# Output, gate and up weights loaded as adjacent rows, with head outputs regrouped on TensorE

## The chip, the cores and the metric

The kernel runs on one core of a Trainium2 chip. A core has TensorE (PE) for matrix products, VectorE (DVE), ScalarE (ACT), GpSimd (POOL) and SyncE (SP), each with its own instruction stream that runs in order, and 16 DMA engines that move data between main memory and the on-chip buffers. Products land in PSUM banks, and everything else lies in SBUF, a memory of 128 partitions. The metric is the device time of one execution in microseconds (us). Three runs of the kernel before took 267.55, 268.86 and 269.77 us.

## The reference: two decoder layers for one token of four sequences

Each of the four rows of x (512 values) passes twice through the same attention block and the same feed-forward block. Both layers use the same weights and the same key and value caches.

```python
B, Sq, D = 4, 1, 512
Hq, Hkv, Sk, Dh = 32, 8, 4096, 128
D, F = 512, 1792
def _A_ref(x, k_cache, v_cache, wq, wo):
    q = (x @ wq) split into 32 heads of 128
    scores = q . k * Dh ** -0.5          # four query heads share one cache head
    o = softmax(scores) . v
    return o.reshape(B, Sq, Hq * Dh) @ wo
def _B_ref(x, w_gate, w_up, w_down):
    return (_gelu(x @ w_gate) * (x @ w_up)) @ w_down

x = x + _A_ref(_layernorm(x), k, v, wq, wo)
x = x + _B_ref(_layernorm(x), w_gate, w_up, w_down)
x = x + _A_ref(_layernorm(x), k, v, wq, wo)
x = x + _B_ref(_layernorm(x), w_gate, w_up, w_down)
```

A sequence's keys are 8 heads of 4096 x 128 in bf16, 1 MB a head, and its values are as large. All in all 64 MB of caches are read at least once, and 13.25 MB of weights: wq and wo with 4 MB each, gate, up and down with 1.75 MB each.

## The kernel before: how the work is tiled, staged and ordered

**Order of the sequences.** The kernel interleaves the layers. `attend_first` runs the attention of layer 1 for sequence 0. Then, for each sequence b, a dense block (`dense_first` or `dense`) runs layer 1's feed-forward part, and `attend` runs layer 2's attention of b, whose keys are still in SBUF, beside layer 1's attention of b+1, whose keys arrive meanwhile. For the last sequence `attend_last` does layer 2's attention alone. The output projection, the feed-forward part of layer 2 and the result (`dense_last`) are done for all four sequences together at the end. So there are four passes with layer-1 attention (the first, and three `attend`) and one last pass.

**Tiles.** A head of a cache is two tiles of 128 partitions x 16 x 128 values (512 KB, 4 KB a partition). Keys are kept whole for a sequence (tiles `kw`, `kp`), and are transposed in place by DVE (L537). Value tiles go through a ring of eight slots (`v_t`): each step of class `Values` uses one tile (`step`, L828), frees its slot, and lets SP issue the next load (`pump`, L708). A few value tiles are kept from layer 1 for layer 2.

**Attention.** `scores` (L592) multiplies keys by a spread query, `soft` takes the softmax over DVE and ACT, `soft_swap` (L647) turns the probabilities on PE, with an ACT copy behind (L650). Values are multiplied in one of two ways: with the tile as weights (L859, output `ot`), or with the probabilities as weights (`stream_v`, L791, output `so`), which DVE then transposes (L799), sums (L806) and scales (L807) into `OT_bf` (layer 1) or `OT2_bf` (layer 2; the profile cuts digits off and writes OT_bf for both). `ot` outputs need one scaling operation (L680). `Values.scale` is that work on DVE; `hold=True` puts it off until `flush`.

**The output projection.** `OT_bf` holds one column a query head, with the 128 values of the head on the partitions. `wo_sb` holds, for head i, the 128 rows of wo that belong to it (`wo_dram`, L102). For most heads `RowProj.heads` (L405) has the head's column as weights and a row block of 512 as moving data, which gives rows; `split` (L412, L413) brings these into bf16 and `onto` adds them through PE to the output `y`. For the last heads `OutProj.heads` (L388) has wo as weights and gives columns. `heads` are four groups of eight query heads, that is, pairs of cache heads, in the order in which they are used.

**What sets the order.** The order of every engine's instructions is that of the program text, written out by hand (`manual_schedule`): `attend_first` (L959), `attend` (L1135) and `attend_last` (L1252) say which step follows which. `busy` (L482) issues filler matmuls whose result nobody reads. All large loads are issued by SP, in program order. `load_rest` (L158) issues wo in four transfers, gate, up and down behind the first pass's values; the first feed-forward block and the keys of sequence 1 follow.

**The dense blocks.** x lies in `xb` and `XX` with 512 = 4 x 128 as (block k, partition p). Gate, up and q have x as weights and a row block of the weight as moving data (L309, L1323, L1390); a DVE transpose (L315) turns rows into columns. In `dense_last`, `row` adds the residual x (and what bf16 cut from it) into `xr` through the identity, and L1440 multiplies down.

## Time and profile before

| | |
|---|---|
| median of three runs | 268.86 us (267.55 to 269.77) |
| the profiled execution's own time | 268.99 us |
| its span, first to last instruction | 267.2 us |
| mean granted TensorE clock | 0.866 of full |
| bytes read | 102.5 MB, 384 GB/s over the span |
| busy: PE, DVE, ACT, POOL | 195.1, 182.2, 66.0, 3.9 us |
| wo: four transfers of 1 MB, rows of 1 KB | 11.0 to 12.9 us from issue to landing |
| packets under 2 KB / all | 7144 / 30732 |

Rows of the timeline read: start, duration (both us), engine, line, operation, output <- inputs, shape, count, and in brackets the idle time of the engine before it and what ended it. Neighbouring instructions of one kind are merged, so a duration can cover short pauses. PEld is the loading of weights, which overlaps PE. Windows give, for each stretch, its length, the busy time of PE, PEld, DVE, ACT and POOL with counts, the granted clock, the DMA engines' busy share and GB/s. The rows of 40 slices cut the span into slices of 6.68 us.

### The profile page before, as it was taken

What the parts mean: (1) busy time and instruction counts of PE and PEld (TensorE: products, weight loads), DVE (VectorE), ACT (ScalarE), POOL (GpSimd) and SP (SyncE); (2) the same over time, 40 slices, a digit from 0 to 9 for tenths busy, and PEclk for the clock granted to TensorE, in tenths of its full rate; (3) what the DMA queues carried; (4) which work ended last, traced back from release to release, by engine and by line L of the source; (5) the groups of instructions that cost most, each with busy time, mean ns of one, the idle gap of its engine ahead of it and who ended that gap; (6) DMA issues with size and microseconds to landing.
All of it is one profiled execution on the core that took longest, in us unless ns stands there. A gap on an engine that the chain in (4) does not pass through costs nothing.

```text
span 267.2 us, 8596 instructions
## 1 busy us (share of the span) xinstructions
PE 195.1 (73%) x3767; PEld 114.8 (43%) x3775; DVE 182.2 (68%) x448; ACT 66.0 (25%) x136; POOL 3.9 (1%) x10
## 2 busy tenths in 40 slices
PE   1396246544689796989678968787788687888884
PEld 1333123322255453557436245464363354553563
DVE  3385955451335899884776998746769996568773
ACT  1001001100222422032323520304136103044642
POOL 2000000000001000000000000000000000000001
PEclk9998555655597959799999985899999979999999
DMA  7999999999994999999999999999999999999940
GB/s 244 432 416 421 423 429 417 408 385 406 413 412 177 394 416 417 420 417 400 390 414 416 416 419 421 416 415 375 403 418 418 421 415 418 420 405 405 413 160 3
DMA packets 30732, 103.05 MB, mean 386 GB/s; under 512 B 2788, under 2 KB 7144, under 8 KB 29672
## 3 DMA queue, kind: packets, MB, share of 16 engines
q1 hardware_dynamic: 30672, 102.51, 95.7%
q8 instruction: 29, 0.48, 0.6%
q14 instruction: 7, 0.06, 0.1%
q10 hardware_dynamic: 24, 0.01, 0.0%
HBM read 102.50 MB, written 0.00 MB: 384 GB/s over the span
## 4 chain that ended last, share of the span: by engine, by line
DMA 51%; PE 21%; DVE 16%; SPq 6%; ACT 3%; issue 3%; DVEq 0%
DMA v_t<-in_A_v_cache_dram 25%; DMA kp<-in_A_k_cache_dram 8%; DMA kw<-in_A_k_cache_dram 8%; PE sc L592 6%; DMA wu_sb<-in_B_w_up_dram 5%; DMA kw<-in_A_v_cache_dram 4%; SPq L161 4%; DVE kp L537 3%; PE ot L859 3%; DVE kw L537 3%; PE y L275 3%; PE so L791 2%; PE q L309 1%; DVE q L315 1%; DVE qb L360 1%
## 5 line engine op out<-in xcount | busy, mean ns | idle before, releaser
L592 PE MATMUL sc<-kw,qb 128*32 128x512 bf16 x244 | 39.6, 446 | 5.2 <-DVE kw L537 2.2
L592 PE MATMUL sc<-kp,qb 128*32 128x512 bf16 x268 | 40.1, 450 | 1.0 <-DVE kp L537 0.2
L592 PEld LDWEIGHTS <-qb 128*32 128x32 bf16 x512 | 23.1, 104 | 39.6 <-issue 21.4
L537 DVE STREAM_TRANSPOSE kw<-kw 128x1024 f32<-128x1024 f32 x32 | 38.0, 1215 | 0.7 <-DMA kw<-in_A_k_cache_dram 0.6
L537 DVE STREAM_TRANSPOSE kp<-kp 128x1024 f32<-128x1024 f32 x32 | 36.7, 1199 | 0.0
L859 PE MATMUL ot<-pe,v_t 128*128 128x32 bf16 (+1 forms) x896 | 30.0, 184 | 5.6 <-DMA v_t<-in_A_v_cache_dram 2.8
L859 PEld LDWEIGHTS <-v_t 128*128 128x128 bf16 x896 | 27.7, 100 | 13.7 <-issue 7.4
L614 ACT ACTIVATE pe<-sc,nl 128x512 bf16<-128x512 f32 x8 | 5.5, 687 | 85.9 <-DVE pe L611 67.6
L791 PE MATMUL so<-v_t,pe 128*32 128x256 bf16 x304 | 15.0, 319 | 13.6 <-DMA v_t<-in_A_v_cache_dram 11.6
L799 DVE STREAM_TRANSPOSE so<-so 128x512 f32<-128x512 f32 (+1 forms) x23 | 13.8, 599 | 11.1 <-PE so L791 11.1
L791 PEld LDWEIGHTS <-pe 128*32 128x32 bf16 x320 | 9.1, 105 | 19.4 <-issue 12.5
L602 DVE TENSOR_REDUCE pe<-sc 128x1 f32<-128x512 f32 x12 | 8.3, 691 | 9.2 <-PE sc L592 9.1
L405 PE MATMUL yr<-wo_sb,OT_bf 128*2 128x512 bf16 (+1 forms) x120 | 10.7, 425 | 4.9 <-DMA wo_sb<-in_A_wo_dram 4.9
L647 PE MATMUL x<-pe,ident_bf 128*32 128x128 bf16 x192 | 5.4, 233 | 11.8 <-DVE pe L622 11.8
L647 PEld LDWEIGHTS <-ident_bf 128*32 128x32 bf16 x256 | 5.3, 100 | 16.1 <-issue 14.1
L791 PE MATMUL so<-v_t,pl 128*32 128x256 bf16 x192 | 9.4, 275 | 3.3 <-DMA v_t<-in_A_v_cache_dram 3.3
L650 ACT CAST pe<-x 128x512 bf16<-128x512 f32 x12 | 7.0, 586 | 17.4 <-PE x L647 17.4
L275 PE MATMUL q<-xb,wq_sb 128*128 128x5 bf16 (+1 forms) x192 | 5.7, 173 | 6.5 <-DMA wq_sb<-in_A_wq_dram 6.5
L353 PE MATMUL qe<-q_bf,ident_bf 128*32 128x16 bf16 (+1 forms) x272 | 5.7, 176 | 5.6 <-DVE q_bf L335 2.9
L622 DVE STREAM_TRANSPOSE pe<-pe 128x512 bf16<-128x512 bf16 x12 | 8.4, 696 | 1.1 <-ACT pe L614 1.1
L275 PEld LDWEIGHTS <-wo_sb 128*128 128x128 bf16 x160 | 7.6, 101 | 3.3 <-DMA wo_sb<-in_A_wo_dram 2.6
L482 PEld LDWEIGHTS <-ident_bf 128*128 128x128 bf16 x63 | 5.2, 99 | 8.7 <-issue 4.3
(172 smaller groups left out, 255.2 us busy)
## 6 DMA issues: line engine op xcount, KB each, us to landing
v_t<-in_A_v_cache_dram SPq DMA_DIRECT2D x89, 512.0 KB, 8.5
kp<-in_A_k_cache_dram SPq DMA_DIRECT2D x32, 512.0 KB, 9.9
kw<-in_A_k_cache_dram SPq DMA_DIRECT2D x24, 512.0 KB, 9.6
wq_sb<-in_A_wq_dram SPq DMA_DIRECT2D x2, 2048.0 KB, 7.7
kw<-in_A_k_cache_dram SPq DMA_DIRECT2D x4, 1024.0 KB, 11.6
v_t<-in_A_v_cache_dram SPq DMA_DIRECT2D x4, 1024.0 KB, 14.2
wo_sb<-in_A_wo_dram SPq DMA_DIRECT2D x4, 1024.0 KB, 12.0
wq_sb<-in_A_v_cache_dram SPq DMA_DIRECT2D x3, 1024.0 KB, 11.8
```

The lines of the kernel that those rows point to most:

```text
L161: dq.dma_start(out=wo_sb[:, i * n:(i + 1) * n], in_=wo_dram[:, i * n:(i + 1) * n])
L275: nc.tensor.matmul(dst, lhsT=lhsT, rhs=rhs, start=first, stop=last, skip_group_check=True)
L405: nc.tensor.matmul(self.rows[j:j + x.shape[1]], lhsT=x, rhs=wo_sb[:, i], start=self.n < QD, stop=True, skip_group_check=True)
L537: nc.vector.transpose(out=words, in_=words)
L592: nc.tensor.matmul(sc[s * QS:(s + 1) * QS], lhsT=qb[:, w0:w0 + 2 * W], rhs=kt[:, :, be // 2, :, be % 2], start=(t == 0 and be == 0), stop= ...
L602: nc.vector.tensor_reduce(out=m, in_=sc.rearrange("p c j -> p (c j)"), axis=AX.X, op=ALU.min if norm else ALU.max)
L622: nc.vector.transpose(out=flat, in_=flat)
L647: nc.tensor.matmul(x[a * QS:(a + 1) * QS, s], lhsT=ident_bf[:, s * QS:(s + 1) * QS], rhs=pT[:, a], start=True, stop=True, skip_group_check ...
L650: nc.scalar.copy(out=pe, in_=x.rearrange("p s t c h -> p (s t c h)"))
L791: nc.tensor.matmul(ps[d, :NW * QS], lhsT=x[:, w:w + NW].rearrange("p c h -> p (c h)"), rhs=v[:, i:i + NW, d], start=first and i == 0, stop ...
L799: nc.vector.transpose(out=flat, in_=flat)
L859: nc.tensor.matmul(self.ot[:, s % 2], lhsT=v[:, i, :], rhs=wide(pe[:, s, t * CH + i, :], self.ot.shape[-1]), start=(done == 0 and i == 0), ...
```

## The change

Loads of wo, gate, up and wq are cut differently, and the order of values in x changes with them.

- In `load_rest`, the output weights of half of the cache heads (those with head mod 4 below 2, two of the four transfers) load with four adjacent rows of wo (4 KB) for a partition: partition p holds rows 4p to 4p+3 of the 512 rows of a cache head's four query heads. The other two transfers stay as they are.
- For those heads the outputs have to lie the same way. A new `Values.regroup` does this: for j in 0 to 3 and each of the four query heads, a matmul of every fourth column of the identity against the head's column writes 32 partitions in PSUM, and an ACT copy brings the result back into `OT_bf` or `OT2_bf`. That is 16 matmuls and a copy for a pair of cache heads. It is called twice in each pass: ahead of the softmax, and between steps or row groups further on.
- Gate and up load with two adjacent rows (7 KB) a partition. So x is kept as (block of 256, partition, even or odd): the out projection and the first pass's down read their weights with a stride of two (`every_other`), later down blocks are read as pairs (`adjacent`), and the residual in `dense_last` is put together from even and odd halves (16 matmuls of 64 columns for 8 of 128). wq loads in two transfers for each half of the heads, its pieces 4 KB as before.
- Some calls change places: in `attend` the third group's rows come in one piece behind the regroup, a filler of five and one of three swap, and in `attend_last` the rows' sum goes between the two halves of the last heads.

```diff
     def load_wq(g):
         n = HG * Dh
-        dq.dma_start(out=wq_sb[g][:], in_=wq_dram[:, :, g * n:(g + 1) * n])
+        for k in range(KD // 2):
+            dq.dma_start(out=by_pairs(wq_sb[g][:])[:, k], in_=wq_dram[:, k, :, g * n:(g + 1) * n])
 
     def load_rest():
         n = Hq // 4
-        for i in range(4):
-            dq.dma_start(out=wo_sb[:, i * n:(i + 1) * n], in_=wo_dram[:, i * n:(i + 1) * n])
-        dq.dma_start(out=wg_sb[:], in_=B_w_gate.rearrange("(k p) n -> p k n", p=P))
-        dq.dma_start(out=wu_sb[:], in_=B_w_up.rearrange("(k p) n -> p k n", p=P))
+        wo_quads = A_wo.rearrange("(i p j) n -> p i j n", p=P, j=QD)
+        to_quads = wo_sb.rearrange("p (i j) n -> p i j n", j=QD)
+        for kvh in range(0, Hkv, 2):
+            if by_quads(kvh):
+                dq.dma_start(out=to_quads[:, kvh:kvh + 2], in_=wo_quads[:, kvh:kvh + 2])
+            else:
+                i = kvh * rep
+                dq.dma_start(out=wo_sb[:, i:i + n], in_=wo_dram[:, i:i + n])
+        dq.dma_start(out=by_pairs(wg_sb[:]),
+                     in_=B_w_gate.rearrange("(k p e) n -> p k e n", p=P, e=2))
...
     class OutProj / RowProj
-                    mac(self.full[:, k], wo_sb[:, i, k * P:(k + 1) * P],
+                    mac(self.full[:, k], wo_sb[:, i, every_other(k)],
...
+        def regroup(self):
+            kvh, n = self.due[0][1][0], sum(len(unit) for _, unit in self.due)
+            ps = self.due[-1][0]
+            self.due = []
+            ...
+            for j in range(QD):
+                for h in range(rep):
+                    nc.tensor.matmul(turned[h * QS:(h + 1) * QS, :, j], lhsT=ident_bf[:, j::QD],
+                                     rhs=o[:, :, h], start=True, stop=True, skip_group_check=True)
+            nc.scalar.copy(out=o, in_=turned)
+
         def scale(self, ot, unit, rden):
             n, s = len(unit), unit[0] % GH
+            if self.quads is not None and by_quads(unit[0]):
+                self.due.append((ot, unit))
...
     attend_first
         vals.step(3, hold=True)
+        vals.regroup()
         p0 = soft(sc1)
...
-        vals.step(TG)
-        assert vals.left() == 0
+        vals.step(2 * NT + 1)
+        vals.regroup()
+        vals.step(vals.left())
         load_rest()
...
     attend
         scores(sc1, gy, 1, last_alone)
+        vals1.regroup()
         p0 = soft(sc1)
...
-        rows.heads(heads[2], rep)
+        vals1.regroup()
+        busy(5, spare)
+        vals1.step(1)
+        rows.heads(heads[2], hp)
+        rows.split()
         busy(3, spare)
-        vals1.step(1)
-        rows.heads(heads[2] + rep, rep)
-        rows.split()
-        busy(5, spare)
         vals1.step(1)
...
     attend_last
+        vals.regroup()
         vals.step(4)
         rows.heads(heads[0], hp)
         rows.heads(heads[1], hp)
+        vals.regroup()
         vals.step(2)
...
         vals.step()
+        proj.n = Hq - rep
+        proj.heads(heads[3] + rep, rep // 2)
         rows.onto(proj)
-        proj.n = Hq - rep
-        proj.heads(heads[3] + rep, rep)
+        proj.heads(heads[3] + rep + rep // 2, rep // 2)
...
     dense_last
         for x in (xb[:], xlo):
             for k in range(KD):
-                row(xr, k, x[:, k, :B], ident_bf[:])
+                half = slice(k % 2 * P // 2, (k % 2 + 1) * P // 2)
+                for e in range(2):
+                    row(xr, k, x[:, k // 2 * 2 + e, :B], ident_bf[:, half], slice(e, P, 2))
```

More of the change, by code (lines that the diff above doesn't have):

```diff
@@ L967, in attend_first @@
                       streamed=[h for h in range(Hkv) if h != last],
-                      paired=[h for h in range(Hkv) if h // 2 != last // 2])
+                      paired=[h for h in range(Hkv) if h // 2 != last // 2],
+                      quads=OT_bf.unsqueeze(2))
         ring.extend(1, b, one(b))
```

36 lines of the change are left out of this document (26 added, 10 removed).

## The prediction

> **What bounds the kernel now.** I read the DMA rows of the page first, then the chain that ended last, then the same time in windows of 2 us, then the timelines of single engines where the diff edits.
>
> ```profile
> DMA  7999999999994999999999999999999999999940
> GB/s 244 432 416 421 423 429 417 408 385 406 413 412 177 394 416 417 420 417 400 390 414 416 416 419 421 416 415 375 403 418 418 421 415 418 420 405 405 413 160 3
> ...
> DMA 51%; PE 21%; DVE 16%; SPq 6%; ACT 3%; issue 3%; DVEq 0%
> ```
>
> The 16 DMA engines are full from 6.7 us to about 256 us, with one hole (slice 13, 80.6 to 84.3 us). So the time is bytes over rate, plus that hole, plus an opening, plus a tail of some 9 us after the last bytes. Only three things can pay: a better rate, a shorter hole, a shorter tail. Work on PE, DVE or ACT elsewhere costs nothing until it makes DMA run dry.
>
> The rate is not the same everywhere. In windows of 2 us (the last two columns are the DMA share and GB/s):
>
> ```profile
> 48.00:50.00 2.00, 1.63 (x34) 1.08 (x34) 0.26 (x1) 1.02 (x2) 0.00 (x0) 0.75 1.03 416
> ...
> 56.00:58.00 2.00, 0.94 (x8) 0.23 (x9) 2.00 (x5) 0.00 (x0) 0.00 (x0) 0.50 1.09 386
> ```
>
> The second window is wo arriving in rows of 1 KB; the first is cache tiles in rows of 4 KB. The engines are as busy or busier, and move 7% less. PE's timeline gives the price exactly, since each group starts as its quarter of wo lands:
>
> ```profile
> 57.06 1.02 PE L405 MATMUL yr<-wo_sb,OT_bf 128*2 128x512 bf16 x8 [1.62 <-DMA wo_sb<-in_A_wo_dram]
> 59.76 1.02 PE L405 MATMUL yr<-wo_sb,OT_bf 128*2 128x512 bf16 x8 [1.68 <-DMA wo_sb<-in_A_wo_dram]
> 62.44 1.02 PE L405 MATMUL yr<-wo_sb,OT_bf 128*2 128x512 bf16 x8 [1.65 <-DMA wo_sb<-in_A_wo_dram]
> 65.16 1.11 PE L275 MATMUL y<-OT_bf,wo_sb 128*128 128x64 bf16 x16 [1.70 <-DMA wo_sb<-in_A_wo_dram]
> ```
>
> 2.70 us a quarter (1.049 MB): 388 GB/s. The gate lands at 69.59 and up at 73.94 (starts of their first readers): 4.43 and 4.35 us for 1.835 MB each, 414 and 422 GB/s, in rows of 3.5 KB.
>
> **What it saves: 0.45 us.** Two quarters of wo go to rows of 4 KB, as the cache tiles have, at 418 GB/s (the steady windows): 2.51 instead of 2.70 us each, 0.4 us for two. Gate and up in rows of 7 KB are bounded by nothing below and by 422 GB/s above: 0.1 us for the gate at most, and I take 0.05. All this lies ahead of the landing of up, from which the chain runs through the first feed-forward block and the first scores to the loads that end the hole. So the hole keeps its length and all behind it comes 0.45 us earlier. The trace has no 4 KB row of wo. Bounds: 0, if the row length is not what costs, and 0.55, at 422 GB/s for all four transfers. The value is nearest to the cache tiles, which have the same row.
>
> The Trainium skill ("DMA: Bandwidth & Descriptors", Specifications) sets line rate at 512 B and up, by which 1 KB rows would lose nothing and this saving would be zero. 388 against 418 GB/s speaks against that. The same page ("Why small descriptors are slow") gives some 3 cycles of overhead for each packet beside one for each 32 B: 35 cycles for 1 KB and 131 for 4 KB, 6% less by an estimate from the page, close to the 7% here.
>
> **What is moved at no cost.** Loading wq in two halves of rows that stay 4 KB: two SP issues more, some 0.45 us each (L156), at the very start, past the key loads and the second half of wq behind them. DMA has over 4 us of work ahead of each. Nothing is gained, since the q matmuls need both halves. Weights read with a stride of two (out projection, down): the trace has such loads for the up projection (LDWEIGHTS of wu_sb, 96 ns) beside contiguous ones of wo_sb (98 ns); equal. Down rows read with a stride: gate rows (strided) take 0.95 us for 16x448, q rows (contiguous) 1.06 us for 16x512; equal for a column. The output's residual rows become 16 matmuls of 64 columns instead of 8 of 128: PE is idle for 0.40 us just behind them (before L1440 at 263.18), and eight more fit (the 56 of that line took 0.95, 0.02 each).
>
> **The regroup, by itself.** 16 matmuls of ident_bf against 2 to 8 columns, then one ACT copy. The nearest row is the spread of q:
>
> ```profile
> 133.25 0.27 PE L353 MATMUL qe<-q_bf,ident_bf 128*32 128x16 bf16 x16 [0.63 <-DVE q_bf L335]
> ```
>
> 0.27 us a regroup. The copy: 0.16 us (L1417, 128x4) to 0.27 us (L1464, 128x128); I take 0.2. What matters is what PE waits for, since PE runs in order and the regroup reads what DVE has just scaled. There are two in each attention pass of layer 1 and two in the last pass.
>
> First pass: the first lies ahead of a 2.03 us idle stretch of PE (45.5 to 47.5), the second after five tiles, ahead of a tile that lands at 51.84, while DVE ends that pair at 51.37. Free.
>
> Passes 2 to 4, first regroup: 0.27 us between scores and fillers, behind which PE is idle 0.78 to 0.97 us for the turned softmax (L647). Its input was ready (L680 at 165.6 against scores' end at 167.5). Free. Second regroup: in the passes that end at 180 and 235 us DVE has ended the second head (175.09, 230.09) as PE gets there, and PE then runs 0.27 of regroup and 0.65 of filler where it had 0.33 of rows and 0.42 of filler, up to a tile at 176.24 and 231.21. Free within 0.1 us. In the pass that ends at 125 us PE arrives at 120.17, DVE ends at 120.46: 0.3 wait, 0.27 of work and the longer filler put the out projection some 0.55 us later. Behind it PE waits on transfers anyway (0.73 at 128.28, 0.59 at 130.83), issued with 5.5 us of other transfers ahead of them. I take 0.1 us for all three; bounds 0 and, if nothing is absorbed, 3 x 0.57 = 1.7.
>
> **The regroups in the last pass: +1.7 us.** Here nothing covers them.
>
> ```profile
> 253.08 0.40 PE L627 MATMUL den<-zx,masks 128*128 128x16 f32 x2
> 253.83 1.06 PE L791 MATMUL so<-wq_sb,pl 128*32 128x256 bf16 x32 [0.36 <-ACT pl L650]
> 254.71 1.04 PE L405 MATMUL yr<-wo_sb,OT_bf 128*4 128x512 bf16 x16
> 255.84 0.62 PE L791 MATMUL so<-wq_sb,pl 128*32 128x256 bf16 x16
> 256.29 0.60 PE L405 MATMUL yr<-wo_sb,OT_bf 128*4 128x512 bf16 x8
> 257.04 0.57 PE L859 MATMUL ot<-pl,kw 128*128 128x32 bf16 x16 [0.15 <-DMA kw<-in_A_v_cache_dram]
> ```
>
> ```profile
> 253.67 0.72 DVE L799 STREAM_TRANSPOSE so<-so 128x512 f32<-128x512 f32 x1
> 254.43 0.22 DVE L806 TENSOR_REDUCE ov<-so 128x8 f32<-128x64 f32 x1
> 254.68 0.18 DVE L807 TENSOR_TENSOR OT_bf<-ov,rden 128x8 bf16<-128x8 f32 x1
> ...
> 259.54 0.18 DVE L425 TENSOR_TENSOR xb<-XX,y 128x16 bf16<-128x16 f32 x1 [0.63 <-PE y L275]
> ```
>
> The first regroup stands ahead of the four V tiles that now start at 253.83. It needs DVE's L807, done at 254.86. Queued behind it on PE: those tiles, then all the rest. On the old clock, with each offset taken from the lines above:
> - regroup 254.9 to 255.2; four tiles start at 255.2 (+1.35); both row groups end at 257.1. The ACT copy sits behind the table load (254.45 to 255.73) and is done by 256.0, in time.
> - DVE scales the next pair from 256.3 for the 1.21 us that it took (254.94 to 256.15): 257.5. So the second regroup waits 0.4 and ends at 257.8. In the kernel before, this scaling lay beside rows and the next tiles.
> - next tiles at 257.75, rows 258.2 to 258.8, DVE's scaling of that head (0.67 after the tiles begin, 0.9 long) ends at 259.3, out projection of it from 259.35; last V tile 259.8 to 260.3; the split of the rows on ACT and DVE (1.1 and 1.7 after the tiles begin, 2.3 until done) ends at 260.2, so the last scale runs from 260.3 to 260.5.
> - 16 matmuls of out projection took 0.59 from start to their DVE reader; with the four of the rows now between them 0.72: xb at 261.3 instead of 259.54.
>
> That is +1.75 us. The cover that the old order had, waits on the last transfers (0.59, 0.66 and 0.21 us on PE, at 255.84, 257.04 and 258.32), is used up in this sum: DMA ends no later, so no term is left for it. Moving the rows' sum behind half of the last heads is 0.1 of it. Bounds: 0.6 us, if only PE's added work and the swapped order stay (2 x 0.27 + 0.1), and 2.2, if the copies come late too (2 x 0.2).
>
> **Sum.** -0.45 + 0.1 + 1.75 = +1.4 us. The profiled execution took 268.99 us with a span of 267.2, so 1.8 lies around the span; 268.99 + 1.4 = 270.4. The median of the three runs shown is 268.86, 0.13 lower; I forecast **270.3 us**, 0.5% slower.
>
> **Rivals.**
> - **The wide rows bring nothing** (the rate of wo comes from elsewhere). Then the saving goes: 270.7. For: the engines' busy share rises to 1.09 in that window without a cause named. Against: gate and up run at 414 to 422 in the same stream. Chance 0.12.
> - **PE's delays reach the transfers.** V loads wait on PE for a free slot; if the second regroup of passes 2 to 4 delays the freed slots and the queue then runs short, each pass loses up to 0.57 us and with the first regroup's 0.27, 0.84: 3 x 0.84 = 2.5 in place of 0.1, 272.7. It decides once a pass loses 0.45 us of transfer time: 1.25 more in all, and over 1% slower. For: the rate sags just there (336 GB/s at 132 us, 295 at 184). Against: 5.5 us of transfers are queued there. Chance 0.13.
> - **Not slower: the hole shortens.** From 79.9 to 83.0 us the granted clock is 0.50, with PE busy all 3.1 us on q and the first scores, on whose end the next loads wait. Had PE the full clock there, as it has from 73 to 79.9, 1.55 us would go and the sum would be -0.15: 268.8. It decides from 1.4 us on, nine tenths of that stretch. For: the drop comes under full load, so its place is not fixed by the work in it. Against: the order of work ahead of it hardly changes. Chance 0.10. The Trainium skill ("TensorE: Matmul & The Clock Gate", Part 1) describes a free-running window of activity of 3.4 us, by which a shift of the work by 0.45 us could fall either way; no run here shows that.
>
> The forecast keeps 0.65. **Range:** from 268.4 (the shortened hole and the low tail cost) to 272.3 (most of the way to the second rival, and the tail's upper bound with no saving: 268.9 + 2.2 + 0.1 = 271.2). The three runs before spread over 2.2 us, so 1% (2.7 us) is about what tells a difference from none. Over 1% slower, above 271.55: the second rival and the upper edge of the tail cost, 0.17. Faster than 266.2: 0.03. Within 1%: 0.80.
>
> **What would show it.** PE's groups that read wo should start 2.5 us apart after the two wide quarters, and 2.7 after the others; up's first reader 0.45 us earlier, and the hole as long as before. In the last pass PE should idle over 1 us ahead of the first regroup with DVE's L807 as its releaser, and the last bytes should land some 0.4 us earlier while xb (add_x) comes over 1 us later. It is wrong if PE does not stall there, if the GB/s row sags more at the passes' ends, or if the granted clock in the hole differs.

## The result: 1.4% slower, not 0.5%

The changed kernel took **272.4 us** (median of six runs, 271.99 to 274.36) against 268.42 us for the kernel before (six runs on the same chip, 267.55 to 270.39): 1.0142 of its time, 95% interval 1.0109 to 1.0174, so 3.8 us more with an interval of 2.9 to 4.7. The forecast was 270.3 us, 1.4 us more. The direction was right, the size was not, and the time lies just above the range. The profiled execution took 274.36 us, span 272.5; it is the slowest of the six, so where its last pass is read, a second profiled execution (272.52 us, span 270.6) stands beside it.

The page of the changed kernel, rows DMA and GB/s of the 40 slices (6.81 us each) and the engines' shares of the chain that ended last:

```profile
DMA  6999999999994999999999999999999999999910
GB/s 155 423 419 420 424 425 419 417 404 414 417 388 168 367 416 417 417 417 417 331 405 419 416 420 417 417 417 405 407 420 415 417 417 418 417 384 385 412 48 3
...
DMA 47%; PE 21%; DVE 18%; SPq 7%; ACT 4%; issue 2%; DVEq 0%
```

The middle is what it was: full, one hole in slice 13. The first slice is new: 155 GB/s where the kernel before had 244. And the bytes end further from the end of the span: 48 GB/s in the second last slice instead of 160, 1.8 us by (160 x 6.68 - 48 x 6.81) / 418.

The two windows again, cache tiles and then wo (length; busy PE, PEld, DVE, ACT, POOL; granted clock; DMA share; GB/s):

```profile
50.00:52.00 2.00, 1.63 (x30) 1.19 (x34) 0.26 (x1) 0.56 (x1) 0.00 (x0) 0.57 1.04 418
58.00:60.00 2.00, 1.02 (x8) 0.23 (x9) 2.00 (x5) 0.00 (x0) 0.00 (x0) 0.50 1.08 406
```

And PE's timeline where the quarters of wo land:

```profile
58.96 1.02 PE L424 MATMUL yr<-wo_sb,OT_bf 128*2 128x512 bf16 x8 [1.47 <-DMA wo_sb<-in_A_wo_dram]
61.52 1.02 PE L424 MATMUL yr<-wo_sb,OT_bf 128*2 128x512 bf16 x8 [1.54 <-DMA wo_sb<-in_A_wo_dram]
64.08 1.02 PE L424 MATMUL yr<-wo_sb,OT_bf 128*2 128x512 bf16 x8 [1.54 <-DMA wo_sb<-in_A_wo_dram]
66.79 1.10 PE L294 MATMUL y<-OT_bf,wo_sb 128*128 128x64 bf16 x16 [1.69 <-DMA wo_sb<-in_A_wo_dram]
```

The quarters that load wide are the first and the third. The third lands 2.56 us after the second (2.49 to 2.56 in the traces of ten executions with wide quarters), where it took 2.68 (2.68 to 2.76 in the eight traces with narrow ones): the saving is there. But the first of these lines comes 1.90 us later than before (57.06): the delay was made ahead of it.

### The profile page after: what moved, and what is told of

Same layout as the page of the kernel before. It is cut to its first block, busy times and chain, and to the rows that moved or that the text cites. A ratio compares the mean times of both kernels' runs of the same rounds, so it can differ in the third digit from the quotient of the medians.

```text
span 272.5 us, 8954 instructions
## 1 busy us (share of the span) xinstructions
PE 195.4 (72%) x3935; PEld 118.4 (43%) x3943; DVE 182.4 (67%) x448; ACT 67.7 (25%) x146; POOL 3.9 (1%) x10
## 4 chain that ended last, share of the span: by engine, by line
DMA 47%; PE 21%; DVE 18%; SPq 7%; ACT 4%; issue 2%; DVEq 0%
DMA v_t<-in_A_v_cache_dram 29%; DMA kp<-in_A_k_cache_dram 7%; PE sc L611 5%; DMA wd_sb<-in_B_w_down_dram 4%; DVE kp L556 4%; DMA kw<-in_A_k_cache_dram 4%; PE so L810 4%; PE ot L879 3%; DVE kw L556 3%; DMA wq_sb<-in_A_wq_dram 3%; PE y L294 2%; SPq L175 2%; PE yr L424 1%; SPq L188 1%; DVE q L334 1%
## 5 line engine op out<-in xcount | busy, mean ns | idle before, releaser
L611 PE MATMUL sc<-kp,qb 128*32 128x512 bf16 x268 | 39.3, 435 | 1.0 <-DVE kp L556 0.2
L424 PE MATMUL yr<-wo_sb,OT_bf 128*2 128x512 bf16 (+1 forms) x120 | 11.4, 466 | 4.5 <-DMA wo_sb<-in_A_wo_dram 4.5
L666 PE MATMUL x<-pe,ident_bf 128*32 128x128 bf16 x192 | 5.1, 226 | 12.2 <-DVE pe L641 12.0
L666 PEld LDWEIGHTS <-ident_bf 128*32 128x32 bf16 x256 | 5.0, 98 | 16.5 <-issue 11.9
L294 PEld LDWEIGHTS <-wq_sb 128*128 128x128 bf16 x192 | 5.4, 101 | 9.1 <-DMA wq_sb<-in_A_wq_dram 8.7
L922 ACT CAST OT_bf<-so 128x8 bf16<-128x8 f32 (+1 forms) x7 | 1.2, 172 | 32.5 <-DVE pe L626 16.4
L810 PEld LDWEIGHTS <-pl 128*32 128x32 bf16 x240 | 5.6, 96 | 8.2 <-issue 6.4
```

The lines of the kernel that those rows point to most:

```text
L294: nc.tensor.matmul(dst, lhsT=lhsT, rhs=rhs, start=first, stop=last, skip_group_check=True)
L424: nc.tensor.matmul(self.rows[j:j + x.shape[1]], lhsT=x, rhs=wo_sb[:, i], start=self.n < QD, stop=True, skip_group_check=True)
L611: nc.tensor.matmul(sc[s * QS:(s + 1) * QS], lhsT=qb[:, w0:w0 + 2 * W], rhs=kt[:, :, be // 2, :, be % 2], start=(t == 0 and be == 0), stop= ...
L666: nc.tensor.matmul(x[a * QS:(a + 1) * QS, s], lhsT=ident_bf[:, s * QS:(s + 1) * QS], rhs=pT[:, a], start=True, stop=True, skip_group_check ...
L810: nc.tensor.matmul(ps[d, :NW * QS], lhsT=x[:, w:w + NW].rearrange("p c h -> p (c h)"), rhs=v[:, i:i + NW, d], start=first and i == 0, stop ...
```

## The opening: where 1.7 us went

Windows of 1 us of three kernels. The kernel before:

```profile
3.00:4.00 1.00, 0.43 (x16) 0.34 (x13) 0.47 (x3) 0.00 (x0) 0.00 (x0) 1.00 0.91 365
4.00:5.00 1.00, 0.00 (x0) 0.00 (x0) 0.19 (x2) 0.00 (x0) 0.69 (x1) 1.00 1.03 418
5.00:6.00 1.00, 0.00 (x0) 0.00 (x0) 0.16 (x1) 0.00 (x0) 0.33 (x1) 1.00 1.03 426
```

The changed kernel:

```profile
3.00:4.00 1.00, 0.38 (x15) 0.29 (x12) 0.49 (x3) 0.00 (x0) 0.00 (x0) 1.00 0.94 176
4.00:5.00 1.00, 0.00 (x0) 0.00 (x0) 0.16 (x1) 0.00 (x0) 0.74 (x1) 1.00 0.83 229
5.00:6.00 1.00, 0.00 (x0) 0.00 (x0) 0.16 (x1) 0.00 (x0) 0.28 (x1) 1.00 0.90 254
```

The experiment `wq_by_e` (below), the changed kernel with another cut of wq's two transfers:

```profile
3.00:4.00 1.00, 0.45 (x16) 0.37 (x14) 0.44 (x3) 0.00 (x0) 0.00 (x0) 1.00 0.89 328
4.00:5.00 1.00, 0.00 (x0) 0.00 (x0) 0.21 (x2) 0.00 (x0) 0.67 (x1) 1.00 1.04 422
5.00:6.00 1.00, 0.00 (x0) 0.00 (x0) 0.16 (x1) 0.00 (x0) 0.36 (x1) 1.00 0.99 406
```

The last two columns are the reading: the DMA engines of the changed kernel are 83 to 94% busy and move 48 to 60% of the bytes that the kernel before moves. They do not wait for an instruction; their packets, pieces of 4 KB in both kernels, take longer. The first MB, which is the first transfer of wq, is slow, and the second transfer behind it runs at 410 GB/s and more. The table gives GB/s in windows of 1 us for the kernels in which the start was varied, and the bytes that had landed by 10 us (sum of the ten windows). `key_first` and `wq_by_e` are made from the changed kernel, so their ratios hold the rest of the change too.

| kernel, first transfer of wq | 2-3 | 3-4 | 4-5 | 5-6 | 6-7 | 7-8 | MB by 10 us | ratio to before, 95% |
|---|---|---|---|---|---|---|---|---|
| before: all rows of a half of the heads, 2 MB | 90 | 365 | 418 | 426 | 418 | 451 | 3.09 | 1 |
| after: rows 0-255, 1 MB | 176 | 176 | 229 | 254 | 274 | 410 | 2.38 | 1.0142 (1.0109 to 1.0174) |
| `wq_split`: rows 0-255 | 156 | 254 | 262 | 225 | 344 | 418 | 2.57 | 1.0066 (1.0030 to 1.0101) |
| `wq_rev`: rows 256-511 | 156 | 229 | 303 | 221 | 365 | 418 | 2.62 | 1.0083 (1.0053 to 1.0114) |
| `wq_rows`: rows 0-255, then their other columns | 152 | 246 | 283 | 213 | 348 | 401 | 2.52 | 1.0056 (0.9975 to 1.0136) |
| `wq_two`: rows 0-255 and 256-511 from two queues | 119 | 332 | 283 | 258 | 348 | 418 | 2.64 | 1.0110 (1.0011 to 1.0209) |
| `key_first`: 1 MB of keys, then rows 0-255 | 214 | 442 | 389 | 406 | 307 | 213 | 2.78 | 1.0101 (1.0072 to 1.0129) |
| `wq_alt`: rows 0-127 and 256-383 | 173 | 418 | 414 | 414 | 426 | 447 | 3.15 | 1.0038 (0.9983 to 1.0092) |
| `wq_by_e`: every second row | 188 | 328 | 422 | 406 | 430 | 447 | 3.12 | 1.0042 (1.0004 to 1.0080) |
| `wq_cols`: all rows, half as many columns | 141 | 399 | 420 | 399 | 418 | 434 | 3.13 | 0.9989 (0.9955 to 1.0024) |

The changed kernel is 0.70 MB behind at 10 us, which is 1.7 us at 418 GB/s, and its second execution (`after_again`) 0.67 MB. Most of that is carried to the last pass: in `after_again` the first key load behind the hole is issued 1.56 us later than before (84.66, before 83.10), and the probability swap of the last pass starts 1.59 us later (254.32, before 252.73).

## The experiments

Line numbers of kernels made from the changed one can be one or two higher than there. All ratios are to the kernel before, run on the same chip in the same batch.

### The whole change again, and the last pass's regroups

`after_again` is the changed kernel unedited. `last_none` leaves out both regroups of `attend_last`, `last_late` moves them to where their input should be ready. `last_none` so leaves out the reordering of layer 2's outputs for the heads with wide weights.

> The changed kernel once more, unaltered, for a second profile. Its first profile lost 2.0 us in the opening (the first q products ended at 12.5 us instead of 10.4, DMA at 176 to 274 GB/s from 2 to 7 us) and was the slowest of six executions (274.36 against a median of 272.4). If the opening belongs to the kernel (wq in two transfers for each half), the first q products end near 12.5 us again. If it was that execution's own, they end near 10.4 us and the span is some 2 us shorter, near 270.5. The tail should be the same in both: from the start of the last probability swap on PE to the last add onto xb 9.3 us, against 6.8 us before.

> Leaves out both regroups of the last pass, so the layer-2 output projection uses columns in the wrong order for half of its heads; all transfers, all other work and the other regroups stay. If the last pass's regroups cost what the first profile shows (2.5 us between the last swap and the add onto xb), the time falls to 270.0 us (272.4 - 2.5). If they cost what was forecast, 1.75 us: 270.7 us. If the loss lies in the opening and in the passes: 272 us. The trade of places between the rows' sum and the last heads stays in, so the swap-to-add stretch should be 6.9 us.

> Both regroups of the last pass put one step later: the first behind the four value tiles (whose scaling is held until then), the second behind the next two. The sum done is the same. If the cost of the regroups is PE's wait on DVE, it falls: the first regroup finds DVE done (254.86 against PE there at 254.9 in the kernel before), and the rows of the second group wait some 0.3 us for the table load and copy, so some 0.7 us of the 2.5 stay and the time is 270.6 us. If the cost is the regroups' own work and the copies, whatever their place, it stays at 272.4 us.

```diff
 # last_none
-        vals.regroup()
         vals.step(4)
         rows.heads(heads[0], hp)
         rows.heads(heads[1], hp)
-        vals.regroup()
 # last_late
-        vals.regroup()
-        vals.step(4)
+        vals.step(4, hold=True)
+        vals.regroup()
+        vals.flush()
         rows.heads(heads[0], hp)
         rows.heads(heads[1], hp)
-        vals.regroup()
         vals.step(2)
+        vals.regroup()
```

Measured: `after_again` 272.83 us, ratio 1.0147 (1.0091 to 1.0202); `last_none` 271.21, 1.0082 (1.0050 to 1.0115); `last_late` 272.25, 1.0134 (1.0072 to 1.0197). The last pass's regroups are worth 0.65% or 1.7 us, near the forecast but with 0.6% of uncertainty either way; the 0.8% that stay without them, more than half of the loss, are elsewhere. Moving them changed 0.13%, less than these intervals can tell.

PE's timeline of `after_again` in the last pass, from the swap (L666) on:

```profile
254.32 0.41 PE L666 MATMUL x<-pl,ident_bf 128*32 128x128 bf16 x16 [0.36 <-DVE pl L641]
254.65 0.39 PE L646 MATMUL den<-zx,masks 128*128 128x16 f32 x2
256.50 0.30 PE L920 MATMUL so<-OT_bf,ident_bf 128*32 128x8 bf16 x16 [1.45 <-DVE OT_bf L826]
256.72 1.06 PE L810 MATMUL so<-wq_sb,pl 128*32 128x256 bf16 x32
257.59 1.05 PE L424 MATMUL yr<-wo_sb,OT_bf 128*4 128x512 bf16 x16
259.08 0.30 PE L920 MATMUL so<-OT_bf,ident_bf 128*32 128x8 bf16 x16 [0.44 <-DVE OT_bf L826]
259.21 0.63 PE L810 MATMUL so<-wq_sb,pl 128*32 128x256 bf16 x16
```

PE stands 1.45 us ahead of the first regroup, which waits for DVE's scaling of the previous pair, and 0.44 us ahead of the second. Both regroups start 2.18 and 4.76 us after the swap (256.50 and 259.08 less 254.32).

DVE's timeline of the same execution gives xb, the sum of x and attention:

```profile
262.82 0.18 DVE L444 TENSOR_TENSOR xb<-XX,y 128x16 bf16<-128x16 f32 x1 [0.75 <-PE y L294]
```

That is 8.50 us after the swap; in the kernel before it was 6.81 (259.54 less 252.73), 1.7 us less. One trace before is not the whole measure: the twelve traces without these regroups take 6.64 to 7.64 us there (mean 7.07), as PE waits 0 to 1.1 us for the last value transfers. So the two regroups make this stretch 0.9 to 1.9 us longer, 1.4 by the mean.

The profiled execution of the changed kernel itself shows the same stretch with something added:

```profile
257.61 0.30 PE L920 MATMUL so<-OT_bf,ident_bf 128*32 128x8 bf16 x16 [1.45 <-DVE OT_bf L826]
257.79 1.26 PE L810 MATMUL so<-wq_sb,pl 128*32 128x256 bf16 x32
258.79 1.96 PE L424 MATMUL yr<-wo_sb,OT_bf 128*4 128x512 bf16 x16
```

The same 16 matmuls of L424 take 1.96 instead of 1.05 us. Windows of that execution give the clock (the column ahead of the DMA share):

```profile
258.00:259.00 1.00, 1.00 (x36) 0.92 (x31) 0.00 (x0) 0.62 (x2) 0.00 (x0) 0.76 1.01 391
259.00:260.00 1.00, 1.00 (x16) 0.35 (x8) 0.88 (x2) 0.00 (x0) 0.00 (x0) 0.50 0.53 199
```

More on that below.

### wq's transfers alone, on the kernel before

> The kernel before, with each half of wq loaded in two transfers of 1 MB (blocks of rows as before, pieces of 4 KB) instead of one of 2 MB; nothing else. If two transfers slow the opening, the first q products end near 12.5 us instead of 10.4 and the time is 270.4 us (268.4 + 2). If the opening of the first profile came from the pairs of rows, or was chance: 268.4 us and 10.4 us.

> The kernel before, each half of wq in two transfers again, but cut by columns: both transfers take all four blocks of 128 rows, in pieces of 2 KB. If the slow opening comes from two transfers in place of one, the first q products end near 12.2 us (10.4 before) and the time is 270.5 us, as with the cut by row blocks (270.64). If it comes from the first transfer's reading only one half of the rows of wq (row blocks 0 and 1, 2 MB of the 4 MB), every transfer now reads over all rows, and the opening is as before: 10.4 us and 268.7 us, some 0.2 us more for the shorter pieces.

```diff
 # wq_split, in load_wq of the kernel before
-        dq.dma_start(out=wq_sb[g][:], in_=wq_dram[:, :, g * n:(g + 1) * n])
+        for k in range(0, KD, 2):
+            dq.dma_start(out=wq_sb[g][:, k:k + 2], in_=wq_dram[:, k:k + 2, g * n:(g + 1) * n])
 # wq_cols
+        for h in range(2):
+            own = slice(h * n // 2, (h + 1) * n // 2)
+            dq.dma_start(out=wq_sb[g][:, :, own], in_=wq_dram[:, :, g * n:(g + 1) * n][:, :, own])
```

Measured: `wq_split` 270.64 us, ratio 1.0066 (1.0030 to 1.0101); `wq_cols` 268.89, 0.9989 (0.9955 to 1.0024). Both issue two DMAs for one. So neither the number of DMAs nor SP's time for a second issue nor the pieces of 2 KB in `wq_cols` cost anything that these intervals show; the cut by row blocks costs 1.8 us (0.8 to 2.7). The table shows that `wq_cols` and the kernel before open alike. `wq_cols` also had the first q products at 9.33 us instead of 10.39 and its time shows no gain from it.

### The change with another cut of wq, and without regroups

> The changed kernel with wq's two transfers cut by even and odd rows instead of by blocks of 256 rows: each transfer reads over all rows of wq, the pieces stay 4 KB, the places in SBUF are the same. If one half of the rows is what slows the opening, the first q products end near 10.4 us and the time falls by 1.8 to 270.8 us. If the number of transfers does, 12.4 us and 272.6 us.

> The changed kernel without any regroup (ten left out: two a pass), so half of the heads meet wo in the wrong order in both layers; all transfers and all other work stay. What is left of the change is the opening (+1.9 by the split alone), the wide rows (-0.3 to -0.45) and the changed places: 270.1 us. Against the run without the last pass's two regroups (271.2) this gives the eight others: 0.1 us was forecast for them, that is 271.1 us here; if the pass that ends at 127 us loses what the profiles show (0.5 to 1 us), 270.2 to 270.7 us.

> The changed kernel with all of wo in rows of 1 KB and so without regroups: what is left is gate, up and wq by pairs and x in pairs. It computes the reference. If the split of wq is all that costs here: 268.7 + 1.9 = 270.6 us, with gate and up landing as far apart as before (4.4 us each). Beside the run without regroups it gives what the 4 KB rows of wo save: 0.3 to 0.45 us by the landings (2.56 us in place of 2.70, twice) and the forecast.

```diff
 # wq_by_e, in load_wq of the changed kernel
-        for k in range(KD // 2):
-            dq.dma_start(out=by_pairs(wq_sb[g][:])[:, k], in_=wq_dram[:, k, :, g * n:(g + 1) * n])
+        for e in range(2):
+            dq.dma_start(out=wq_sb[g].rearrange("p (k e) n -> p k e n", e=2)[:, :, e],
+                         in_=wq_dram[:, :, e, g * n:(g + 1) * n])
 # no_regroup: the six calls of regroup (ten executions) are left out
 # pairs_only: the same, and no wide wo, so that nothing has to be regrouped
     def by_quads(kvh):
-        return kvh % GH < 2
+        return False
```

Measured: `wq_by_e` 270.67 us, ratio 1.0042 (1.0004 to 1.0080); `no_regroup` (which leaves out the reordering in both layers) 270.23, 1.0042 (1.0005 to 1.0079); `pairs_only` 270.82, 1.0051 (1.0017 to 1.0084). Another cut of wq gives back 1.0% and the opening of the kernel before; leaving out all regroups gives back as much. `pairs_only` keeps the slow opening and has neither wide wo nor regroups: its 1.4 us (0.5 to 2.3) are within what the opening alone costs in `wq_split` (1.8), so gate and up in rows of 7 KB show no gain.

### The parts one by one, without the slow opening

> The changed kernel with wq's halves cut by even and odd rows (so that each of their transfers reads from all rows of wq) and with none of the ten regroups; what it computes is therefore not the reference's output for the heads whose weights are loaded four rows wide. What is left of the change is the wide rows of wo, gate and up, the strided reads and the order of steps. Theory (the opening costs 1.8 us, the wide wo saves 0.3 to 0.45): 270.23, as without regroups, less 1.8, that is 268.4; or the kernel before (268.9) less 0.3 to 0.45, 268.5 to 268.6. Rival 1, the wide rows bring nothing: 268.9 to 269.0. Rival 2, the order of steps and the strided reads cost something of their own: over 269.3.

> As the kernel beside it, but with the eight regroups of passes 1 to 4 put back; only the two of the last pass are left out, so the heads of layer 2 that they serve come out in the wrong order. The difference to the kernel with none is the price of these eight. By the prediction 0.1 us: 268.5 if the other gives 268.4. By the difference of the two earlier kernels without and with them (271.21 less 270.23) 1.0 us: 269.4. And what the kernel with all ten regroups and this cut of wq took (270.67) less this one is the price of the last pass's two: 1.75 by the prediction, so 268.9; if this kernel takes 269.4 the last pass costs only 1.2.

> The change whole, in the best form found: wq's halves cut by even and odd rows, and the regroups of the last pass put behind the four tiles and behind the second row group's place, where their DVE input is ready. With all of wq's slow opening gone (1.8 us) and the last pass at +1.0 instead of +1.6: 272.5 less 2.4, 270.1 us. If the later place gave only what it gave before (272.25 against 272.6), 270.3. Below 268.9 only if the saving of wo were larger than read from its landings.

```diff
 # by_e_none: wq_by_e, and no call of regroup
 # by_e_passes: wq_by_e, and in attend_last
-        vals.regroup()
         vals.step(4)
...
-        vals.regroup()
         vals.step(2)
 # by_e_late: wq_by_e with the edit of last_late
```

Measured, with the ratio taken as us of 268.7:

| kernel | median | ratio, 95% | to before | step |
|---|---|---|---|---|
| `by_e_none`: wide rows, no regroup | 268.17 | 0.9974 (0.9943 to 1.0005) | -0.7 us | wide rows: -0.7 |
| `by_e_passes`: and eight regroups | 268.72 | 0.9996 (0.9964 to 1.0028) | -0.1 | eight regroups: +0.6 |
| `wq_by_e`: and the last pass's two | 270.67 | 1.0042 (1.0004 to 1.0080) | +1.1 | last two: +1.2 |
| after: and wq cut by row blocks | 272.4 | 1.0142 (1.0109 to 1.0174) | +3.8 | wq's cut: +2.7 |

The first step has 0.8 us of uncertainty (one interval), the others 1.2 to 1.4 (two intervals beside each other), so only the sign of the last is certain from this table alone. By medians the steps are -0.5, +0.55, +1.7 and +2.3. `by_e_late`, the whole change in the best form found, took 269.85 us, ratio 1.0032 (1.0002 to 1.0061): still not faster. No version of the whole change beats the kernel before.

The wide rows work: PE's timeline of `by_e_none` has the narrow second quarter 2.69 us after the first and the wide third 2.52 us after that.

```profile
57.09 1.02 PE L425 MATMUL yr<-wo_sb,OT_bf 128*2 128x512 bf16 x8 [1.46 <-DMA wo_sb<-in_A_wo_dram]
59.78 1.02 PE L425 MATMUL yr<-wo_sb,OT_bf 128*2 128x512 bf16 x8 [1.67 <-DMA wo_sb<-in_A_wo_dram]
62.30 1.02 PE L425 MATMUL yr<-wo_sb,OT_bf 128*2 128x512 bf16 x8 [1.49 <-DMA wo_sb<-in_A_wo_dram]
```

The first regroup of a pass is covered, as forecast. In `by_e_passes` PE comes to the swap of the second pass after 0.61 us of idling; in `by_e_none`, which has no regroup ahead of it, after 0.78 us, with DVE's turned softmax as releaser both times. First `by_e_passes`, then `by_e_none`:

```profile
115.32 0.41 PE L667 MATMUL x<-pe,ident_bf 128*32 128x128 bf16 x16 [0.61 <-DVE pe L642]
```

```profile
115.89 0.41 PE L667 MATMUL x<-pe,ident_bf 128*32 128x128 bf16 x16 [0.78 <-DVE pe L642]
```

In `by_e_late` the first regroup comes behind the four tiles and waits for nothing; the second still makes the row group behind it wait, now for ACT's copy:

```profile
253.46 1.06 PE L811 MATMUL so<-wq_sb,pl 128*32 128x256 bf16 x32 [0.37 <-ACT pl L670]
254.54 0.30 PE L921 MATMUL so<-OT_bf,ident_bf 128*32 128x8 bf16 x16
254.68 1.54 PE L425 MATMUL yr<-wo_sb,OT_bf 128*4 128x512 bf16 x16
256.05 0.61 PE L811 MATMUL so<-wq_sb,pl 128*32 128x256 bf16 x16
256.48 0.27 PE L921 MATMUL so<-OT_bf,ident_bf 128*32 128x8 bf16 x16
257.11 0.60 PE L425 MATMUL yr<-wo_sb,OT_bf 128*4 128x512 bf16 x8 [0.35 <-ACT OT_bf L923]
```

There xb follows the swap after 7.62 us (259.98 less 252.36), and in the trace of `last_late` too (262.66 less 255.04): 0.9 us less than the 8.50, and as much as the longest of the traces without these regroups.

### What makes the opening slow

> The changed kernel with one head of keys (two transfers of 512 KB, contiguous in memory) loaded ahead of wq instead of behind it; wq's halves stay cut by row blocks. Theory A, only the first transfer's reading from half of wq's rows while the queue starts is slow: the keys run at over 350 GB/s from about 2.5 us, wq behind them at over 400, and the time is 272.6 less 1.8, 270.8 us. Theory B, any transfer of a narrow part of memory is slow for the first 6 us: keys at 150 to 260 GB/s, and 272.6 or more. Theory C, wq's half rows are slow wherever they stand in the first 8 us: the keys are fast, then the rate falls to some 200 GB/s, and 272.0 to 272.6.

> The kernel before, each half of wq loaded in two transfers by row blocks as in the slow form (two of the four blocks of 128 rows each), but the blocks 2 and 3 (rows 256 to 511) ahead of the blocks 0 and 1. Theory A, a transfer that reads from a narrow half of wq's rows is slow if it is the first: again 150 to 260 GB/s until 1.05 MB have landed at about 6 us, first q products read at about 12.2 us, 270.4 us. Theory B, the slowness belongs to rows 0 to 255 or their memory: the first transfer runs at 400 GB/s and the second is the slow one.

> The kernel before, each half of wq in two transfers of two row blocks, but alternate ones: blocks 0 and 2 (rows 0 to 127 and 256 to 383), then 1 and 3. Theory A, what counts is that one transfer reaches over all of wq's rows: full rate from 3 us on (365 to 430 GB/s), q products read at 9.5 to 10.5 us, 268.7 us. Theory C, what counts is that a partition has two pieces in a transfer instead of four, at a distance of whole blocks: slow as with adjacent blocks, q at 12.2 us, 270.4 us.

> The kernel before, each half of wq in two transfers by adjacent row blocks (the slow cut), the second of the two issued by ACT, so that both run at the same time from two queues. Theory A, slow because only one half of the rows is read at a time: full rate, q products read at 9.5 to 10.5 us, 268.7 us. If the cut itself is slow however it is mixed: 150 to 260 GB/s, q at 12 us, 270.4 us.

> The kernel before, wq loaded at the start in four transfers of 1 MB: rows 0 to 255 of the first half of the heads, rows 0 to 255 of the second half, then rows 256 to 511 of both; the keys come behind all of them, so the first q products wait for 3 MB and the time itself says little. Theory A1, only the first transfer is slow, since it meets engines that start in step: 150 to 260 GB/s up to about 6 us, full rate behind it. Theory A2, reading only these 256 rows is slow for as long as nothing else is read: 150 to 260 GB/s for the first two transfers, up to about 10 us.

```diff
 # key_first, in attend_first of the changed kernel
+        keys.load_heads(1)
         load_wq(gx)
-        keys.load_heads(GH)
+        keys.load_heads(GH - 1)
 # the others, in load_wq of the kernel before, with blocks of 128 rows
 # wq_rev: as wq_split, blocks 2 and 3 first
+        for k in (2, 0):
 # wq_alt: blocks 0 and 2, then 1 and 3
+        for k in range(2):
+            dq.dma_start(out=wq_sb[g][:, k::2], in_=wq_dram[:, k::2, g * n:(g + 1) * n])
 # wq_two: as wq_split, the second transfer issued by ACT
+            (dq if k == 0 else nc.scalar).dma_start(...)
 # wq_rows: blocks 0 and 1 of one half of the heads, of the other half,
 # then blocks 2 and 3 of both; keys behind
```

Measured: `key_first` 271.44 us, 1.0101 (1.0072 to 1.0129); `wq_rev` 270.36, `wq_alt` 269.69, `wq_two` 271.07, `wq_rows` 270.40, with the ratios of the table (two or three runs each; the openings tell more than the times).

- `wq_rev`: rows 256 to 511, put first, are as slow as rows 0 to 255. It is not one part of memory.
- `wq_rows`: only the first of the four transfers is slow; rows 0 to 255 of the other columns, read next, run at 401 GB/s and more from 7 us on. It is not reading these rows as such either. Nor is it reading only one half of the rows at a time: the second transfer of `wq_split`, rows 256 to 511 alone, runs at 418 to 459 GB/s from 7 to 9 us.
- `wq_alt`: two blocks of 128 rows that are not adjacent run at 414 and more from 3 us on, with the same number of pieces and bytes as `wq_split` (its time, 1.0038, can't be told from that of the kernel before). What counts is that the transfer covers a closed block of 256 rows; all of these transfers take half of each row, so whether that matters too is not shown.
- `wq_two`: it does not show what two halves read at once would do. ACT issued its two transfers from 1.3 us on, but up to 6.5 us its DMA queue (q10) moved only the row of x, while SP's queue (q1) moved 1.19 MB (packets, MB, share of the engines):

```profile
q1 hardware_dynamic: 283, 1.19, 66.5%
q10 hardware_dynamic: 8, 0.00, 0.4%
```

  So the first transfer of wq was again the only one of wq that ran, at 258 to 348 GB/s from 4 to 7 us. Later both queues move bytes, from 8 to 9 us:

```profile
q1 hardware_dynamic: 33, 0.27, 63.7%
q10 hardware_dynamic: 36, 0.15, 35.8%
```

  The Trainium skill ("DMA: Bandwidth & Descriptors", Issuing engines are not separate DMA queues) says that transfers issued by different engines run on the same 16 DMA engines and interleave; the trace agrees from 6.5 us on, not before. DVE read the first q products at 16.55 us, against 12.14 in `wq_split`: the second transfer shared the engines with the keys.
- `key_first`: the keys (one transfer of 1 MB, not the two of 512 KB of the expectation) open at full speed (442 GB/s), and wq's first transfer behind them sags all the same, for some 2 us instead of 4:

```profile
5.00:6.00 1.00, 0.00 (x0) 0.00 (x0) 0.00 (x0) 0.00 (x0) 0.94 (x1) 1.00 1.02 406
6.00:7.00 1.00, 0.00 (x0) 0.00 (x0) 0.16 (x1) 0.00 (x0) 0.09 (x1) 1.00 1.03 307
7.00:8.00 1.00, 0.00 (x0) 0.00 (x0) 0.00 (x0) 0.00 (x0) 0.00 (x0) 1.00 0.95 213
8.00:9.00 1.00, 0.00 (x0) 0.00 (x0) 0.00 (x0) 0.00 (x0) 0.00 (x0) 1.00 0.94 348
```

So the empty queue at the start is not the whole cause, but it makes it worse: `key_first` is 0.31 MB behind at 10 us, the changed kernel 0.70. What is shown is the form (the first transfer that reads wq, if it covers a closed block of half its rows) and the price. Why the packets take longer there was not settled.

## Why the forecast failed, by its own steps

**"What is moved at no cost: loading wq in two halves" failed.** It was costed at nothing, because DMA had over 4 us of work ahead of each DMA and the pieces stayed at 4 KB. The pieces did stay at 4 KB, and `wq_cols` shows that a second issue costs nothing, but that does not answer the question: the rate of a transfer depended on which rows it gathers, not on the size of its pieces or on SP. The trace before could have warned in one way only: wq was read there at 365 to 426 GB/s from 3 us on, and that was the rate of another access pattern. In its place the runs show +1.8 us for that cut alone on the kernel before (`wq_split`, 0.8 to 2.7) and +2.7 as the last step of the table; the landed bytes account for 1.7 us in the changed kernel. This step had no bounds, and so the range had none for it.

**"Two quarters of wo go to rows of 4 KB": right.** 2.51 us was forecast for a wide quarter, 2.49 to 2.56 was measured, 0.34 us for two by a mean of 2.53 (at 422 GB/s the upper bound comes to 0.51 us, not to the 0.55 of the forecast). `by_e_none` has 0.7 us less than the kernel before (1.5 less to 0.1 more), which takes in the forecast 0.45. Gate and up were taken at 0.05: the landings from the last quarter of wo to up are 8.86 us (66.79 to 75.65) where they were 8.78, so nothing. The rival that the wide rows bring nothing is not what happened for wo.

**"The regroups in the last pass: +1.7": right in its steps, the size known to about 0.5 us.** The forecast times put the first regroup 2.17 us and the second 4.77 us after the swap and xb 8.57 us after it; `after_again` shows 2.18, 4.76 and 8.50. The sum took its reference from one trace; against the twelve traces without these regroups the stretch is 0.9 to 1.9 us longer. In time the two are worth 1.2 us by the ratios of `by_e_passes` and `wq_by_e` and 1.7 us by `last_none` and `after_again`, with over 1 us of uncertainty either way. DVE's scaling, which used to run beside other work of PE, became the wait, at the line named (L807 there, L826 here).

**"0.1 us for all three" later passes: too small by what can't be resolved.** Eight regroups cost 0.6 us by the table, with bounds of about -0.6 and 1.8; the forecast's bounds were 0 and 1.7. The rival in which PE's delays reach the transfers asked for 2.5 us there, and that is outside.

**"So the hole keeps its length": its end kept its place in the chain, its start did not.** The keys that end the hole are issued 4.34 us after the second xb before (83.10 less 78.76), 4.25 and 4.35 us in the two traces of the changed kernel. But DMA runs dry earlier ahead of it. From 72 to 98 us the kernel before moved 347 GB/s, the changed one 329 (and 332 in `after_again`): 4.4 us of transfers at 418 GB/s are missing there before, 5.5 and 5.3 us after. First before, then after:

```profile
72.00:98.00 26.00, 22.41 (x445) 13.75 (x447) 17.52 (x48) 8.17 (x15) 1.16 (x2) 0.83 0.88 347
72.00:98.00 26.00, 22.27 (x450) 13.51 (x450) 16.11 (x46) 8.17 (x15) 1.17 (x2) 0.83 0.86 329
```

The rival of the shorter hole asked for the full clock. It did not happen in the two traces of the changed kernel: the granted clock is 0.50 for 3.4 us there as before (79.7 to 83.1 before, 81.0 to 84.4 and 81.3 to 84.7 after). But this drop does not go with the change or with its opening. Of the eighteen traces of this case six have it (these three, `last_late`, `pairs_only` and `wq_rows`), and twelve do not, among them `no_regroup`, which has all the loads of the changed kernel. SP's timelines show the price in the issue of the first keys behind the hole: `before` (drop), `by_e_none` (no drop), the changed kernel (slow opening and drop), `no_regroup` (slow opening, no drop):

```profile
83.10 3.20 SPq L518 DMA_DIRECT2D kp<-in_A_k_cache_dram  x5
82.08 3.17 SPq L538 DMA_DIRECT2D kp<-in_A_k_cache_dram  x5
84.71 3.16 SPq L537 DMA_DIRECT2D kp<-in_A_k_cache_dram  x5
83.69 3.17 SPq L537 DMA_DIRECT2D kp<-in_A_k_cache_dram  x5
```

| first keys behind the hole, us | clock 1.00 | clock 0.50 for 3.4 us |
|---|---|---|
| opening as before or cut over all rows | 81.47 to 82.21 (6 traces) | 83.10 (1) |
| slow opening | 83.52 to 83.69 (5) | 84.43 to 84.87 (5) |

(`key_first`, with its half-slow opening and no drop, is at 82.43.) So at this point the slow opening costs 1.5 to 1.75 us by the means, and the drop 1.0 to 1.2, where the forecast took 1.55 for it. How often each kernel has the drop in executions without a trace is not known, so a part of each difference of medians can come from it; single traces are to be compared within a column.

**The sum.** With the terms that were measured in traces: opening +1.7, wide rows -0.3, eight regroups +0.6 (from the table), last pass +1.4 (0.9 to 1.9), together +3.4 of 3.8 us. That agreement is better than the parts are known: the pass behind the first dense block is 0.5 to 1.0 us longer in the changed kernel's two traces than before (xb to xb 47.26 and 46.71 us, against 46.24 before and 46.00 in `wq_by_e`). `pairs_only` takes 46.86 us for it without any regroup, so the regroups are not needed for it. It lies behind the hole: from the issue of the first keys there to the xb that ends the pass the eighteen traces take 41.90 to 43.01 us, the kernel before the least of all, the changed kernel the most (and 42.36 in `after_again`). What sets this spread is not shown. The sag in slice 20 of the changed kernel (331 GB/s) is no proof for the regroups: `no_regroup` has 337 GB/s there.

## What to carry to other kernels

A load that is cut in two keeps its bytes and its piece size, and can still change its rate: ask which addresses one transfer gathers, and compare the GB/s of the first microseconds, where nothing else is in the queue, before calling a cut free. If a load has to be cut, cut it so that each part still reaches over the whole weight (by columns, by every second row or by alternate blocks); here that was the difference between nothing and 1.8 us. And work added behind an engine that runs in order costs what it waits for, not what it takes: ten regroups of 0.3 us each cost little where PE waited anyway, and by the medians most of their price came from the two in the pass without cover. Last, before two traces are compared stage by stage, compare their granted clock in that stage: here it moved a stage by 1.0 to 1.2 us between traces.

## What the runs showed of the hardware that was not expected

- A transfer of 1 MB out of a closed block of 256 rows of 8 KB (4 KB of each) ran at 176 to 303 GB/s from 3 to 6 us when it was the first to read wq, with the DMA engines 83 to 104% busy (the changed kernel, `wq_split`, `wq_rev`, `wq_rows`); the same bytes in alternate blocks or rows ran at 406 and more from 4 us on, and a second transfer of the same form right behind it at 400 and more.
- Rows of 1 KB instead of 4 KB cost 6% of the rate (2.70 us for 1.049 MB against 2.53), and from 3.5 to 7 KB nothing more was gained.
- After 1.45 us of PE idling in the last pass, the granted clock fell to 0.50 for 3.4 us in two of the four profiled executions with the regroups in that place (from 258.5 to 261.9 us in the changed kernel, from 255.4 to 258.8 in `wq_by_e`), and not in `after_again` and `key_first`; xb came 9.28 and 9.74 us after the swap instead of 8.50 in both of these. In the kernel before and the other thirteen traces without that idling it did not fall between the swap and xb. The Trainium skill ("TensorE: Matmul & The Clock Gate", Why this matters for your kernels) warns of gaps above some 3 us between bursts of matmuls; here a gap of half that, with work on both sides, was followed by the drop. That it was the cause is not shown, only that the drop came there in half of the executions.
- A drop to 0.50, again for 3.4 us, also came while PE was busy all of the time: at the hole, in six of eighteen traces.
- A transfer that ACT issued at 1.3 us (`wq_two`) moved nothing until 6.5 us, while the first transfer of SP's queue was in work.
